# Rounded weight halves on ScalarE, a reordered first batch and a planner with measured durations, in a fused attention and expert kernel

## The chip, the cores and the metric

The kernel runs on one core of a Trainium2 chip. The metric is the device time of one execution in microseconds; lower is better. TensorE (PE) multiplies, VectorE (DVE) and ScalarE (ACT) do elementwise work, GpSimd (POOL) does some of it and issues accumulating DMAs, SyncE (SP) issues the other DMAs.

## What is computed

Two stages. First an attention over 8 batches, 8 heads, 576 positions and 64 features per head: a coarse attention on q, k and v averaged over groups of four positions, repeated four times, plus a local one in which each position sees those less than four away. Then a feed-forward stage on the 4608 rows of 512 features, with a rational activation.

```python
q_d = q.reshape(B, H, Sd, factor, D).mean(axis=3)      # k_d, v_d alike
out_d = sm_attn(q_d, k_d, v_d)
out_up = np.repeat(out_d, factor, axis=2)
mask = np.abs(pos[:, None] - pos[None, :]) < factor
...
out_local = np.matmul(attn, v)
x = (out_up + out_local), rows b*576+s, columns h*64+d
h = x @ w_in                                  # 512 -> 2048
P = a[0] + a[1] * h + a[2] * h2 + a[3] * h3
Q = 1.0 + np.abs(b[0]) * np.abs(h) + np.abs(b[1]) * h2
out = (P / (Q + 1e-06)) @ w_out               # 2048 -> 512
```

The weights come as 64-bit numbers, so that a chunk of 128 x 512 of them is 512 KB.

## The kernel before

**Planner.** Nothing is issued at once. Each piece of work is a task given to `Plan.add` (line 86) with an engine, a duration, what it reads and writes, and sometimes a due time. `Plan.run` (line 117) walks back from due times to a latest time for each task, then simulates five engines: whenever an engine is free, it takes, of its tasks that are ready by the simulated clock, the one with the earliest latest time. The result is a fixed order per engine; on the chip each engine works through its list in order, and waits where an input is not there. An engine is never held free for a task that will be ready soon. `gap` gives the time from the end of a task to the start of one that depends on it; a DMA on SP counts as 2.0 us after its issue, one on POOL as given by `lag`.

**Weights.** There are 16 chunks of w_in and 16 of w_out (`weights`, line 303). A chunk is loaded as raw words into one of eleven landing buffers (`spots`), which lie over memory used later: five over the buffers of the activation, four over the last two chunks' places, two over x. ScalarE scales one word (line 320), VectorE puts the two words together into a float (lines 323 and 326), which is kept in the place `low`. `parts` (line 337) then splits it in two: POOL rounds the high part (line 340), VectorE subtracts it to leave the low part (line 343). For w_out this follows at once; for w_in it waits until block 0 has used the whole float.

**Attention.** A batch has four pairs of heads. A pair needs qk (590 KB), vw (the windows of v, 320 KB), and pooled qk and v. For batches 1 to 7 the pooling is done by DMA: one load and three accumulating loads from POOL (line 376). For batch 0 VectorE pools qk (line 387), and v of all four pairs is pooled by one load and three accumulating ones into one buffer `vf` (lines 807 and 811). Then: scores (lines 399, 409, 426), maxima on VectorE (441, 471), exponentials on ScalarE (456, 482), normalization on VectorE (493 to 517), transposes (530, 537), copies on ScalarE (543, 553, 554), products with v (`weighted`, lines 568 and 579), and additions that put the result into x (line 611). Batch 0 is worked in two halves of two pairs; its loads on SP are interleaved with the first six weight chunks by due times. Pairs 2 and 3 of batch 0 use memory that lies over places of later chunks.

**Feed-forward.** Rows come in blocks: 512 rows of a batch, and twice 256 rows left over from four batches. A block has 16 steps (8 for the small ones), 144 steps in all. A step has `h_part` (x by one chunk of w_in), `middle` (the activation: six ScalarE operations at line 705 and seven VectorE operations at lines 720 to 738) and, two steps later, `o_part` (by one chunk of w_out, line 757). Block 0 takes w_in and x as whole floats, four slow matmuls to a step (line 680); later blocks take high and low parts, three products, twelve matmuls (line 692); for that `split_x` first splits x (lines 659 and 662). h has two PSUM banks, the output four, so that the third h step needs the first bank emptied by `middle`. The due time of step n is `due_h(n)`: `H0` for the first, `H_FIRST` more for each step of block 0 and `H_STEP` afterwards. A block's x is due `SPLIT_EARLY` before its first step. Batch 1's attention runs during block 0.

**Filling.** Where the plan leaves PE idle before the first h step, `warm` puts in matmuls with no use (line 889), for 0.6 of the planned gap.

Of the kernel before, what the change touches and what calls it, by code (L numbers as in the profile page):

```python
# [20 lines left out]
P = 128  # L21
# [51 lines left out]
class Task:  # L73
    __slots__ = ("engine", "dur", "fn", "due", "preds", "succs", "late", "start", "end", "n", "lag")


class Plan:

    LAG = {"PE": 0.25, "DVE": 0.14, "ACT": 0.18, "POOL": 0.2, "SP": 2.0}
    OWN = {"PE": 0.0, "DVE": 0.08, "ACT": 0.1, "POOL": 0.1, "SP": 2.0}
# [6 lines left out]
    def add(self, engine, dur, fn, reads=(), writes=(), due=None, lag=None):  # L89
        t = Task()  # L90
        t.engine, t.dur, t.fn, t.due, t.n = engine, dur, fn, due, len(self.tasks)
        t.lag, t.preds, t.succs, t.late, t.start = lag, {}, [], 1e9, None
# [11 lines left out]
        for k in rk - wk:  # L104
            self.readers[k].append(t) if k in self.readers else self.readers.__setitem__(k, [t])
# [6 lines left out]
    def gap(self, p, t):  # L112
        if p.lag is not None:
            return p.lag
        return (self.OWN if p.engine == t.engine else self.LAG)[p.engine]

    def run(self):
# [6 lines left out]
        waiting = {e: [] for e in self.LAG}  # L124
        open_ = {e: [] for e in self.LAG}
        free = dict.fromkeys(self.LAG, 0.0)

        def release(t):
            at = 0.0
# [7 lines left out]
        done = []  # L137
        while len(done) < len(self.tasks):
            best = None
            for e in self.LAG:  # L140
                if open_[e]:
                    at = free[e]
                elif waiting[e]:
                    at = max(free[e], waiting[e][0][0])
                else:
                    continue
                if best is None or at < best[0]:
                    best = at, e
            at, e = best
            while waiting[e] and waiting[e][0][0] <= at + 1e-9:  # L150
                t = heapq.heappop(waiting[e])[2]
                heapq.heappush(open_[e], (t.late, t.n, t))
            t = heapq.heappop(open_[e])[2]
# [14 lines left out]
def attention_moe(  # L168
# [95 lines left out]
    slots += [Slot(2 + i, high[i][half].at) for i in range(2)]  # L264
    vf = put("vf", [KC, NPAIR, 2, 2, D], F32, low[0][half].at)
# [3 lines left out]
    spots += [put(f"sl{i}", [P, 2 * DM], I32, a[w][NFC - 2].at) for i, (a, w) in enumerate(((high, 0), (low, 0), (high, 1), (low, 1)))]  # L269
    spots += [put(f"sx{i}", [P, 2 * DM], I32, xs[1][0].at + i * 4096) for i in range(2)]  # L270
# [23 lines left out]
    add("SP", 0.4, lambda: nc.sync.dma_start(out=maskb.ap, in_=mask), (), (maskb,), due=-20.0)  # L294

    def setup_coef():
        add("SP", 0.1, lambda: nc.sync.dma_start(out=cf.ap[:, :6], in_=coef), (), (cf,), due=30.0)
# [7 lines left out]
    def weights(w, f, spot, due=None):  # L305
# [25 lines left out]
        add("SP", 1.4, load, (), (spot,), due=due)  # L331
# [3 lines left out]
        if w:  # L335
            parts(w, f)

    def parts(w, f, due=None):
        hi, lo, word = high[w][f], low[w][f], bits[w][f]
        add("POOL", 1.0, lambda: nc.gpsimd.tensor_copy(out=hi.ap, in_=word.ap.bitcast(F32)), (lo,), (hi,), due=due)  # L340
# [19 lines left out]
    def load_qk(c, due=None):  # L360
        s, b, i = c.slot, c.b, c.i
        add("SP", 1.6, lambda: nc.sync.dma_start(out=s.qk.ap, in_=qk[b, i]), (), (s.qk,), due=due)

    def load_vw(c, due=None):
        s, b, i = c.slot, c.b, c.i
        add("SP", 0.9, lambda: nc.sync.dma_start(out=s.vw.ap, in_=vw[b, i]), (), (s.vw,), due=due)

    def load_pooled(c):

        s, b, i = c.slot, c.b, c.i  # L370
        for dst, src, cost in ((s.pq, qkp, 0.5), (c.vp, vp, 0.4)):
            add("SP", cost, lambda d=dst, x=src: nc.sync.dma_start(out=d.ap, in_=x[b, 0, :, i]), (), (dst,))
            for r in range(1, POOL):
                add(
                    "POOL", 1.0,
# [3 lines left out]
                    (dst,), (dst,), lag=2.8,  # L379
# [11 lines left out]
    def scores(c, bk):  # L391
# [24 lines left out]
        add("PE", 1.0, issue, (s.qk, identb, maskb), bk)  # L416

    def scores_pooled(cs, bk):
# [14 lines left out]
        add("PE", 0.9, issue, [c.slot.pq for c in cs], bk)  # L433
# [122 lines left out]
    def vp_of(c):  # L556
        return vf.ap[:, c.i] if c.b == 0 else c.vp.ap

    def weighted(cs, bk, due):
# [15 lines left out]
        def part_b():  # L575
            for c, x in zip(cs, avb):
                for kc in range(2):
                    for j in range(2):
                        nc.tensor.matmul(  # L579
                            x.ap[j * D : (j + 1) * D, 256 : 256 + SD],  # L580
                            lhsT=vp_of(c)[:, j, kc, :],
                            rhs=c.slot.ept.ap[:, kc, :, c.pos(j), :],
                            start=(kc == 0), stop=(kc == 1), skip_group_check=True,
# [10 lines left out]
        pooled_v = [vf if c.b == 0 else c.vp for c in cs]  # L594
# [25 lines left out]
        add("PE", 1.4 if len(cs) == 2 else 0.87, part_b, [c.slot.ept for c in cs] + pooled_v + ready, avb)  # L620
# [11 lines left out]
        add("PE", 0.95, part_a, ready, ava)  # L632
# [35 lines left out]
    def h_part(n, f):  # L668
# [5 lines left out]
        if k == 0:  # L674

            x = xsf[blk.slot][1]
            for c in range(NCC):
# [7 lines left out]
                add("PE", 0.88, issue, (low[0][fc], part(x, None, 4 * c * t, 4 * t)), (ph,), due=due_h(n) + 0.05 * c)  # L685
# [21 lines left out]
    def middle(n):  # L707
# [20 lines left out]
        act(0.54, tq, log, log.ap, AF.Exp, scale=-1.0)  # L728
        add("DVE", 0.61, lambda: v.tensor_tensor(out=gh.ap, in0=ta.ap, in1=tq.ap, op=ALU.mult), (ta, tq), (gh,))  # L729
# [10 lines left out]
    def o_part(n, f):  # L740
# [5 lines left out]
        due = due_h(n) + O_LAG * H_STEP + 0.25 * f  # L746
        order = [[(m, sub) for m in range(3)] for sub in range(blk.nsub)]
# [21 lines left out]
    def store(k):  # L769
        blk = blocks[k]  # L770
        due = due_h(blk.first + blk.nstep + 2)
        for sub in range(blk.nsub):
# [9 lines left out]
            for i, (b, t, n) in enumerate(rows):  # L782
# [5 lines left out]
                    (room,), (), due=due + 2,  # L788
# [4 lines left out]
    spot_of = [spots[i % 9] for i in range(9)] + [spots[5 + i % 4] for i in range(len(order) - 9)]  # L793
    late = [i for i, (w, f) in enumerate(order) if f >= NFC - 2]
    for n, i in enumerate(range(late[0], len(order))):
        spot_of[i] = spots[9 + n % 2]
    chunks = [(w, f, spot) for (w, f), spot in zip(order, spot_of)]


    c0 = [Pair(p) for p in range(NPAIR)]  # L800
    due0 = due_h(0) - 4.0
# [5 lines left out]
    add("SP", 0.8, lambda: nc.sync.dma_start(out=vf.ap, in_=vp[0, 0]), (), (vf,), due=-18)  # L807
    for r in range(1, POOL):
        add(
            "POOL", 1.0,  # L810
            lambda r=r: nc.gpsimd.dma_start(out=vf.ap, in_=vp[0, r], accum_op=ALU.add),
            (vf,), (vf,), lag=4.0,
        )
    early = (-16, -13, -10, -9, -7, -5)
    for (w, f, spot), due in zip(chunks[: len(early)], early):
        weights(w, f, spot, due)
    bk = banks
    for q in range(2):
        cs = c0[2 * q : 2 * q + 2]
        for i, c in enumerate(cs):  # L820
            scores(c, bk[2 * i : 2 * i + 2])
            softmax_local(c, bk[2 * i : 2 * i + 2])
        for c in cs:
            pool_qk(c)
        sp = bk[4:6] if q == 0 else bk[0:2]
        scores_pooled(cs, sp)
        for c, y in zip(cs, sp):
            softmax_pooled(c, y)
        for i, c in enumerate(cs):
            normalize(c)  # L830
            turned(c, [bk[n] for n in ((6, 4, 5), (6, 4, 5), (2, 3, 0), (6, 1, 2))[2 * q + i]])
        weighted(cs, [bk[n] for n in ((4, 5, 4, 5), (1, 2, 0, 3))[q]], due0 - 10.0 * (1 - q))
    for w, f, spot in chunks[len(early) :]:
        weights(w, f, spot)

    def attend(b):
# [145 lines left out]
```

## Time and profile before

| | us |
|---|---|
| median of 3 runs | 995.44 (995.34 to 995.81) |
| profiled execution, span | 992.7 |
| first h step of block 0 starts | 47.03 |
| block 1 starts | 178.56 |
| last PE matmuls start | 986.25 |

The profile is one execution on the chip. Its page gives busy times of the engines, the span in 40 slices, and groups of instructions by line; the trace behind it can be asked for stretches, instructions in order of time, and waits. L680 is line 680. Matmul records overlap, so a pitch is taken from start to start. A task's records carry the line of the operation, so L705 stands for all six ScalarE operations of the activation. Rows of DMA queues show bytes and the time to landing.

### The profile page before, as it was taken

To read this page: it belongs to the slowest core of one execution; us is meant where nothing else is said; L and a number is where in the kernel's file an instruction comes from. 1 tells how busy PE (TensorE), PEld (TensorE's weight loads), DVE (VectorE), ACT (ScalarE), POOL (GpSimd) and SP (SyncE) were. 2 spreads that over 40 slices of the span, in tenths; PEclk is the share of its full clock that TensorE was granted. 3 is DMA by queue.
4 is the path that set the end of the run, shared out by engine and by line. 5 is a ranking of instruction groups with operands and counts; after the bars stand their busy time and mean duration, and the time that the engine had idled before them with its cause. 6 is when DMAs were issued, how large, how long until landed. Compare 5 with 4: busy or idle time off the path is not lost.

```text
span 992.7 us, 19799 instructions
## 1 busy us (share of the span) xinstructions
PE 961.0 (97%) x7365; PEld 758.1 (76%) x7365; DVE 849.1 (86%) x1472; ACT 796.6 (80%) x2046; POOL 180.4 (18%) x209
## 2 busy tenths in 40 slices
PE   6689998999999999999999999999999999999997
PEld 5545665788888878987878887887878888898886
DVE  6799999989778988887887898888888898888886
ACT  6578768797979798779787988798797979767675
POOL 1523543222221213001303030302122220000000
PEclk9999999999999999999999999999999999999999
DMA  9963553433342324002424242533334320100001
GB/s 322 281 210 120 118 158 70 117 68 74 74 125 51 74 74 84 34 22 74 75 72 96 85 80 59 95 96 56 92 57 112 74 52 1 44 1 22 1 1 42
DMA packets 46371, 83.43 MB, mean 84 GB/s; under 512 B 6564, under 2 KB 29092, under 8 KB 46276
## 3 DMA queue, kind: packets, MB, share of 16 engines
q1 hardware_dynamic: 25828, 62.70, 19.1%
q0 software_dynamic: 20448, 19.48, 14.1%
q8 instruction: 58, 0.95, 0.4%
q14 instruction: 37, 0.30, 0.1%
HBM read 72.72 MB, written 9.44 MB: 83 GB/s over the span
## 4 chain that ended last, share of the span: by engine, by line
PE 82%; DVE 10%; DMA 4%; issue 2%; POOL 1%; SPq 1%; ACT 1%; ACTq 0%; DVEq 0%; POOLq 0%
PE psum L757 36%; PE psum L692 36%; PE psum L568 2%; DMA pq<-in_qkp_dram 2%; PE psum L579 1%; PE psum L530 1%; PE psum L537 1%; PE psum L409 1%; PE psum L426 1%; DMA qk<-in_qk_dram 1%; DVE m L720 1%; DMA sx<-in_w_out_dram 1%; DVE m L726 1%; POOL wh L340 1%; DVE g L729 1%
## 5 line engine op out<-in xcount | busy, mean ns | idle before, releaser
L757 PE MATMUL psum<-wh,g 128*128 128x512 f32 x1152 | 371.7, 403 | 4.7 <-DVE g L738 2.7
L692 PE MATMUL psum<-xs,wh 128*128 128x512 f32 (+1 forms) x1152 | 265.2, 370 | 0.0
L705 ACT ACTIVATE m<-psum,cf 128x512 f32<-128x512 f32 x288 | 217.5, 759 | 51.9 <-PE psum L692 41.9
L757 PEld LDWEIGHTS psum<-wh,g 128*128 128x128 f32 x1152 | 209.3, 188 | 55.5 <-issue 7.7
L692 PEld LDWEIGHTS psum<-xs,wh 128*128 128x128 f32 x1152 | 199.3, 188 | 35.9
L757 PE MATMUL psum<-wl,g 128*128 128x512 f32 x576 | 225.0, 392 | 0.0
L705 ACT ACTIVATE gb<-psum,cf 128x512 f32<-128x512 f32 x144 | 115.7, 803 | 53.9 <-PE psum L757 53.7
L376 POOL DMA_DIRECT2D pq<-in_qkp_dram x84 | 73.9, 913 | 398.3 <-DMA pq<-in_qkp_dram 312.5
L692 PE MATMUL psum<-xs,wl 128*128 128x512 f32 (+1 forms) x576 | 141.5, 367 | 0.0
L729 DVE TENSOR_TENSOR g<-m,m 128x512 fp32r<-128x512 f32 x144 | 100.6, 699 | 43.2 <-ACT m L705 41.3
L720 DVE SCALAR_TENSOR_TENSOR m<-m,cf,m 128x512 f32<-128x512 f32 x144 | 108.9, 756 | 31.2 <-ACT m L705 31.1
L757 PEld LDWEIGHTS psum<-wl,g 128*128 128x128 f32 x576 | 108.4, 188 | 23.4
L456 ACT ACTIVATE el<-psum,nm 128x64 f32<-128x64 f32 x320 | 97.0, 345 | 30.4 <-DVE nm L448 30.1
L726 DVE TENSOR_TENSOR m<-m,gb 128x512 f32<-128x512 f32 x144 | 101.7, 706 | 20.3 <-ACT gb L705 16.3
L692 PEld LDWEIGHTS psum<-xs,wl 128*128 128x128 f32 x576 | 101.3, 189 | 18.9 <-issue 1.2
L705 ACT ACTIVATE gb<-m,cf 128x512 f32<-128x512 f32 x144 | 107.0, 743 | 6.3 <-DVE m L720 6.3
L732 DVE SCALAR_TENSOR_TENSOR m<-m,g 128x512 f32<-128x512 f32 x144 | 100.0, 695 | 2.9
L737 DVE TENSOR_TENSOR m<-m,m 128x512 f32<-128x512 f32 x144 | 99.2, 689 | 2.8
L376 POOL DMA_DIRECT2D vp<-in_vp_dram x84 | 72.7, 925 | 154.5 <-DMA vp<-in_vp_dram 136.8
L725 DVE TENSOR_TENSOR m<-m,m 128x512 f32<-128x512 f32 x144 | 98.5, 684 | 0.5 <-ACT m L705 0.5
L738 DVE TENSOR_TENSOR g<-m,m 128x512 fp32r<-128x512 f32 x144 | 97.9, 680 | 0.8
L705 ACT ACTIVATE m<-gb 128x512 f32<-128x512 f32 x144 | 93.6, 650 | 3.5 <-DVE m L725 0.9
(66 smaller groups left out, 999.0 us busy)
## 6 DMA issues: line engine op xcount, KB each, us to landing
qk<-in_qk_dram SPq DMA_DIRECT2D x32, 590.0 KB, 8.0
pq<-in_qkp_dram POOLq DMA_DIRECT2D x84, 144.0 KB, 3.3
vw<-in_vw_dram SPq DMA_DIRECT2D x32, 320.0 KB, 4.0
out_dram<-xf SPq DMA_DIRECT2D x32, 256.0 KB, 2.4
vp<-in_vp_dram POOLq DMA_DIRECT2D x84, 72.0 KB, 3.0
sl<-in_w_in_dram SPq DMA_DIRECT2D x10, 512.0 KB, 4.7
sl<-in_w_out_dram SPq DMA_DIRECT2D x10, 512.0 KB, 6.3
pq<-in_qkp_dram SPq DMA_DIRECT2D x28, 144.0 KB, 2.2
```

Source lines behind the costliest of these rows:

```text
L376: lambda d=dst, x=src, r=r: nc.gpsimd.dma_start(out=d.ap, in_=x[b, r, :, i], accum_op=ALU.add),
L456: nc.scalar.activation(out=s.el.ap[:, k, c.pos(j), :], in_=view[:, j, k, :], func=AF.Exp, bias=nm[:, 5 * j + k : 5 * j + k + 1], scale=sca ...
L692: nc.tensor.matmul(ph.ap[:, f * t : (f + 1) * t], lhsT=(high, low)[j][0][fc].ap[:, c, :], rhs=blk.x[i].ap[:, c, :], start=(part_ == 0 and ...
L705: add("ACT", cost, lambda: nc.scalar.activation(out=out_.ap, in_=in_, func=func, **kw), (room_in, cf, *more), (out_,))
L720: lambda: v.scalar_tensor_tensor(out=tb.ap, in0=tq.ap, scalar=b1, in1=tb.ap, op0=ALU.mult, op1=ALU.add),
L725: add("DVE", 0.61, lambda: v.tensor_tensor(out=ta.ap, in0=ta.ap, in1=tq.ap, op=ALU.mult), (ta, tq), (ta,))
L726: add("DVE", 0.61, lambda: v.tensor_tensor(out=ta.ap, in0=ta.ap, in1=u.ap, op=ALU.add), (ta, u), (ta,))
L729: add("DVE", 0.61, lambda: v.tensor_tensor(out=gh.ap, in0=ta.ap, in1=tq.ap, op=ALU.mult), (ta, tq), (gh,))
L732: lambda: v.scalar_tensor_tensor(out=tb.ap, in0=tb.ap, scalar=CONE, in1=gh.ap.bitcast(F32), op0=ALU.add, op1=ALU.mult),
L737: add("DVE", 0.61, lambda: v.tensor_tensor(out=tb.ap, in0=ta.ap, in1=tb.ap, op=ALU.subtract), (ta, tb), (tb,))
L738: add("DVE", 0.61, lambda: v.tensor_tensor(out=gl.ap, in0=tb.ap, in1=tq.ap, op=ALU.mult), (tb, tq), (gl,))
L757: nc.tensor.matmul(ob[sub].ap, lhsT=g[i].ap[:, f0 : f0 + P], rhs=flat((high, low)[j][1][fc].ap), start=(fc == 0 and m == 0), stop=(fc == N ...
```

## The change

- **High parts.** `parts` rounds the high part with a ScalarE copy instead of a GpSimd one; planned duration 0.5 instead of 1.0.
- **First batch.** All qk loads come first, then pooled v, then vw, then the weight chunks; there are no due times on them. Pooled v goes into two buffers, each by one load and one accumulating load, and the product sums over both. The pairs are worked one at a time, each with banks given by `FIRST`, and due `PAIR_GAP` apart.
- **Planner.** Durations are changed to other values, DMAs get a delay that follows their size, an engine is free from 0.7 on. New is the hold: where a task of earlier latest time (by `HOLD_MARGIN`) will be ready before 0.7 of the chosen task has passed, the engine takes a ready task that fits in the time until then, or is left free; this up to a planned time of 54.4.
- **Landing buffers.** The two over x go; the four shared ones now lie over the high places of w_in chunks 14, 5, 3 and 1 (and each one's successor).
- **Batch 1's loads** are not planned before 45 (first two pairs) and 75 (others).
- **Due times** are changed by constants. The code for `n < WHOLE` (w_out as whole floats in the first steps) is there, with WHOLE = 0.

```diff
-        add("POOL", 1.0, lambda: nc.gpsimd.tensor_copy(out=hi.ap, in_=word.ap.bitcast(F32)), (lo,), (hi,), due=due)
+        add("ACT", 0.5, lambda: nc.scalar.copy(out=hi.ap, in_=word.ap.bitcast(F32)), (lo,), (hi,), due=due)
...
-        if p.lag is not None:
-            return p.lag
+        if p.load is not None:
+            return 2.05 if p.engine == "SP" else 1.8 + 1.3 * p.load
...
-            t = heapq.heappop(open_[e])[2]
+            t = ready[e][0][2]
+            urgent = None
+            for r, _, w in waiting[e]:
+                if r < at + t.dur * HOLD and w.late < t.late - HOLD_MARGIN and (urgent is None or w.late < urgent[0]):
+                    urgent = w.late, r
+            if urgent is not None and at < HOLD_UNTIL:
+                fits = [x for x in ready[e] if at + x[2].dur <= urgent[1] + 0.05]
+                if not fits:
+                    free[e] = urgent[1]
+                    continue
+                x = min(fits)
+                ready[e].remove(x)
+                heapq.heapify(ready[e])
+                t = x[2]
...
-    slots += [Slot(2 + i, high[i][half].at) for i in range(2)]
-    vf = put("vf", [KC, NPAIR, 2, 2, D], F32, low[0][half].at)
+    slots += [Slot(2 + i, high[i][half - 1].at) for i in range(2)]
+    vf = [put(f"vf{i}", [KC, NPAIR, 2, 2, D], F32, low[0][half + 2 * i].at) for i in range(2)]
...
-    spots += [put(f"sl{i}", [P, 2 * DM], I32, a[w][NFC - 2].at) for i, (a, w) in enumerate(((high, 0), (low, 0), (high, 1), (low, 1)))]
-    spots += [put(f"sx{i}", [P, 2 * DM], I32, xs[1][0].at + i * 4096) for i in range(2)]
+    spots += [put(f"sl{i}", [P, 2 * DM], I32, high[0][(NFC - 2, half - 3, half - 5, half - 7)[i]].at) for i in range(4)]
...
-        add("SP", 1.4, load, (), (spot,), due=due)
+        add("SP", 1.28, load, (), (spot,), due=due, load=1.28)
...
-                for kc in range(2):
+                terms = [(v, kc) for kc in range(2) for v in vp_of(c)]
+                for n, (v, kc) in enumerate(terms):
...
-    for c, due in zip(c0, (-19, -17, -15, -12)):
-        load_qk(c, due)
-    for c, due in zip(c0, (-14, -11, -8, -6)):
-        load_vw(c, due)
+    for c in c0:
+        load_qk(c)
+    for r in range(POOL):
+        v = vf[r // 2]
+        if r % 2:
+            add(
+                "POOL", 0.93, lambda r=r, v=v: nc.gpsimd.dma_start(out=v.ap, in_=vp[0, r], accum_op=ALU.add),
+                (v,), (v,), load=1.3,
+            )
+        else:
+            add("SP", 0.8, lambda r=r, v=v: nc.sync.dma_start(out=v.ap, in_=vp[0, r]), (), (v,), load=0.8)
+    for c in c0:
+        load_vw(c)
...
-    for q in range(2):
-        cs = c0[2 * q : 2 * q + 2]
...
+    for i, c in enumerate(c0):
+        sc, sp, tb, av = FIRST[i]
+        scores(c, [banks[n] for n in sc])
+        softmax_local(c, [banks[n] for n in sc])
+        pool_qk(c)
+        scores_pooled([c], [banks[sp]])
+        softmax_pooled(c, banks[sp])
+        normalize(c)
+        turned(c, [banks[n] for n in tb])
+        weighted([c], [banks[n] for n in av], due_h(0) - 1.0 - PAIR_GAP * (NPAIR - 1 - i))
...
-                load_qk(c), load_pooled(c), load_vw(c)
+                at = HOLD_LOADS[q] if b == 1 else 0.0
+                load_qk(c, at), load_pooled(c, at), load_vw(c, at)
...
-                    parts(0, n, due_h(n + blocks[0].nstep) - 2.0)
+                    parts(0, n, due_h(n + blocks[0].nstep) - PARTS_EARLY)
...
-H0 = 40.0
-H_FIRST = 8.0
+H0 = 36.0
+H_FIRST = 6.73
 H_STEP = 6.2
-SPLIT_EARLY = 6.0
+SPLIT_EARLY = 9.51
+PARTS_EARLY = 14.42
 QUAD_GAP = 45.0
+PAIR_GAP = 3.53
+COEF = 16.26
+HOLD = 0.7
+HOLD_MARGIN = 2.06
+HOLD_UNTIL = 54.4
 WARM = 0.6
+WHOLE = 0
+HOLD_LOADS = (45.0, 75.0)
```

More of the change, by code (lines that the diff above doesn't have):

```diff
@@ L73 @@
 class Task:
-    __slots__ = ("engine", "dur", "fn", "due", "preds", "succs", "late", "start", "end", "n", "lag")
+    __slots__ = ("engine", "dur", "fn", "due", "preds", "succs", "late", "start", "end", "n", "load", "at")
 class Plan:
-    LAG = {"PE": 0.25, "DVE": 0.14, "ACT": 0.18, "POOL": 0.2, "SP": 2.0}
-    OWN = {"PE": 0.0, "DVE": 0.08, "ACT": 0.1, "POOL": 0.1, "SP": 2.0}
+    ENGINES = ("PE", "DVE", "ACT", "POOL", "SP")
+    LAG = {"PE": 0.25, "DVE": 0.14, "ACT": 0.18, "POOL": 0.2}
+    OWN = {"PE": 0.0, "DVE": 0.08, "ACT": 0.1, "POOL": 0.1}
     def __init__(self):
@@ L123, in run @@
         left = {t: len(t.preds) for t in self.tasks}
-        waiting = {e: [] for e in self.LAG}
-        open_ = {e: [] for e in self.LAG}
-        free = dict.fromkeys(self.LAG, 0.0)
+        waiting = {e: [] for e in self.ENGINES}
+        ready = {e: [] for e in self.ENGINES}
+        free = dict.fromkeys(self.ENGINES, 0.7)
+        done = []
         def release(t):
-            at = 0.0
+            at = t.at
             for p in t.preds:
@@ L136, in run @@
                 release(t)
-        done = []
         while len(done) < len(self.tasks):
             best = None
-            for e in self.LAG:
-                if open_[e]:
+            for e in self.ENGINES:
+                if ready[e]:
                     at = free[e]
@@ L334, in weights @@
         add("DVE", 0.6, lower, (spot, lo), (lo,))
-        if w:
+        if w and f >= WHOLE:
             parts(w, f)
@@ L618, in put_x @@
             )
[L620 removed]
+        add("PE", 1.6, part_b, [c.slot.ept for c in cs] + pooled_v + ready, avb)
         for c, x in zip(cs, avb):
@@ L746, in o_part, with issue @@
         due = due_h(n) + O_LAG * H_STEP + 0.25 * f
+        if n < WHOLE:
+            x = gb[n % 2]
+            for sub in range(blk.nsub):
+                def issue(sub=sub):
+                    nc.tensor.matmul(
+                        ob[sub].ap, lhsT=x.ap[:, sub * P : (sub + 1) * P], rhs=flat(bits[1][fc].ap).bitcast(F32),
+                        start=(fc == 0), stop=False,
+                    )
+                add("PE", 0.858, issue, (x, low[1][fc]), (ob[sub],), due=due + 0.02 * sub)
+            return
         order = [[(m, sub) for m in range(3)] for sub in range(blk.nsub)]
@@ L787, in store @@
                     ),
-                    (room,), (), due=due + 2,
+                    (room,), (), due=due + 2, load=0.7,
                 )
     order = sorted(((w, f) for w in range(2) for f in range(NFC)), key=lambda c: c[1] / 2 + 1.5 * c[0])
[L793 to L796, printed above, removed]
@@ L833, in attention_moe @@
-    for w, f, spot in chunks[len(early) :]:
+    chunks = [(w, f, spots[i if i < 9 else 5 + (i - 9) % 4]) for i, (w, f) in enumerate(order)]
+    c0 = [Pair(p) for p in range(NPAIR)]
+    for c in c0:
[3 more added lines that the diff above has]
+        if r % 2:
+            add(
+                "POOL", 0.93, lambda r=r, v=v: nc.gpsimd.dma_start(out=v.ap, in_=vp[0, r], accum_op=ALU.add),
+                (v,), (v,), load=1.3,
+            )
+        else:
+            add("SP", 0.8, lambda r=r, v=v: nc.sync.dma_start(out=v.ap, in_=vp[0, r]), (), (v,), load=0.8)
@@ L874, in attention_moe @@
                 o_part(o, f)
+                if k == 0 and o < WHOLE:
+                    parts(1, o, due_h(o + blocks[0].nstep) + O_LAG * H_STEP - PARTS_EARLY)
             if s == blocks[k].nstep - 1:
```

93 lines of the change are left out of this document (43 added, 50 removed), and 4 rows, old and new, of the table FIRST.

## The prediction

> **What bounds the kernel now.** I read the page first, its busy times and its slices; then the table by stretches; then TensorE's instructions in order of time, to place the cuts; then what ScalarE, VectorE and GpSimd did there; last, the instruction groups.
>
> ```profile
> span 992.7 us, 19799 instructions
> PE 961.0 (97%) x7365; PEld 758.1 (76%) x7365; DVE 849.1 (86%) x1472; ACT 796.6 (80%) x2046; POOL 180.4 (18%) x209
> PE   6689998999999999999999999999999999999997
> ```
>
> 97% for PE is an average. The slices show where the remainder is: at the start, and a little at the end. The stretches are cut where the first h step starts (47.03), where the third starts (59.06), where the last h step of block 0 ends (162.5) and where block 1 starts (178.56). The columns are PE, PEld, DVE, ACT and POOL busy, then granted clock, DMA share and GB/s.
>
> ```profile
> 0.00:47.03 47.03, 32.07 (x561) 23.96 (x562) 33.31 (x72) 29.88 (x136) 14.53 (x24) 1.00 0.95 301
> 47.03:59.06 12.03, 9.64 (x60) 4.29 (x60) 9.20 (x17) 5.88 (x10) 4.26 (x6) 0.86 1.05 334
> 59.06:162.50 103.44, 98.06 (x572) 58.25 (x572) 101.83 (x179) 83.50 (x227) 41.14 (x41) 1.00 0.47 127
> 162.50:178.56 16.06, 12.58 (x138) 9.59 (x137) 15.43 (x28) 11.13 (x23) 3.82 (x5) 0.89 0.35 64
> 47.03:178.56 131.53, 120.28 (x769) 72.13 (x769) 126.46 (x221) 100.52 (x258) 49.23 (x50) 0.97 0.51 138
> 178.56:992.70 814.14, 808.67 (x6037) 661.99 (x6035) 689.31 (x1181) 666.20 (x1652) 116.65 (x136) 1.00 0.27 63
> ```
>
> ```profile
> 47.03 8.80 PE L680 MATMUL psum<-xf,wb 128*128 128x512 f32 x16 [3.89 <-DVE xf L611]
> 59.06 7.23 PE L680 MATMUL psum<-xf,wb 128*128 128x512 f32 x16 [2.38 <-ACT gb L705]
> 178.56 2.88 PE L692 MATMUL psum<-xs,wh 128*128 128x512 f32 x12
> ```
>
> From 178.56 on PE is busy 808.67 of 814.14 us, and its work there is the same after the change. So the question is **how much earlier block 1 starts**. Before it VectorE is the full engine: 101.83 of 103.44 in the long middle stretch. PE itself does real work at this rate:
>
> ```profile
> 95.65 3.59 PE L680 MATMUL psum<-xf,wb 128*128 128x512 f32 x8
> 184.00 0.62 PE L757 MATMUL psum<-wh,g 128*128 128x512 f32 x2
> 186.72 1.98 PE L692 MATMUL psum<-xs,wh 128*128 128x512 f32 x8
> ```
>
> An h step of block 0 is the eight records of the first row, 3.59 us; an o step is the twelve matmuls between the other two, 2.72 us.
>
> **The change part by part.**
>
> *First batch ahead of the weights, pair by pair.* On SP, ten loads (four qk, four vw, two of pooled v) and two accumulating loads on POOL go ahead of every chunk load. By the DMA view of the first 48 us (count, size, us to landing) they are 4 x (590 + 320 + 288) KB = 4.8 MB:
>
> ```profile
> qk<-in_qk_dram SPq DMA_DIRECT2D x6, 590.0 KB, 8.5
> vw<-in_vw_dram SPq DMA_DIRECT2D x6, 320.0 KB, 11.8
> vf<-in_vp_dram POOLq DMA_DIRECT2D x3, 288.0 KB, 7.8
> ```
>
> At the first stretch's 301 GB/s that is 16 us, so the first chunk lands near 18 us. That costs nothing: h needs it only after 35 us, and it has twenty us of cover. What is removed shows on VectorE, and where ScalarE starts:
>
> ```profile
> 8.65 0.31 ACT L456 ACTIVATE el<-psum,nm 128x64 f32<-128x64 f32 x1 [6.64 <-DVE nm L448]
> 17.43 1.35 DVE L387 TENSOR_REDUCE pq<-qk 128x288 f32<-128x1152 f32 x1 [1.74 <-DMA qk<-in_qk_dram]
> 40.95 0.69 DVE L343 TENSOR_TENSOR wl<-wb,wh 128x512 fp32r<-128x512 f32 x1 [2.22 <-POOL wh L340]
> 42.50 1.07 DVE L323 TENSOR_SCALAR wb<-sx 128x512 int32<-128x512 int32 x1
> 46.32 1.67 DVE L611 TENSOR_TENSOR xf<-psum,up 128x48 f32<-128x48 f32 x6
> ```
>
> The fourth pair's qk came 1.74 us late; VectorE stood 2.22 us at a subtraction whose POOL cast was not done; and 3.82 us of weight work (42.50 to 46.32) ran ahead of the additions that give h its x. Together 7.8 us, which puts the first h step at 39.2. Bounds: nothing, and from below ScalarE, which starts its exps at 8.65 and is busy 29.88 us up to 47.03, 1.3 of them a table load and 6.8 ten chunk scalings (0.68 each); 8.65 + 21.8 + 1.7 for the last additions = 32 us, a gain of 15. I take 7.8, the waits I can name. Pooled v in two buffers adds 16 matmuls of about 0.075 us (sixteen take 1.20 at L579), beside idle PE, and shortens three loads in sequence, which nobody waits for at the end: zero.
>
> *The first two h steps.* They took 12.03 us where two steps are 7.2. TensorE was at half clock, and ScalarE, in order, stood at chunk scalings whose loads were late before it could empty the first h bank:
>
> ```profile
> 48.00:49.00 1.00, 1.00 (x2) 0.37 (x2) 0.65 (x2) 0.28 (x1) 0.82 (x1) 0.50 0.87 303
> 47.61 0.67 ACT L320 ACTIVATE sl<-sl 128x512 f32<-128x512 f32 x1 [5.28 <-DMA sl<-in_w_out_dram]
> 55.91 0.70 ACT L320 ACTIVATE sx<-sx 128x512 f32<-128x512 f32 x1 [1.40 <-DMA sx<-in_w_out_dram]
> 56.52 0.66 ACT L705 ACTIVATE m<-psum,cf 128x512 f32<-128x512 f32 x1
> ```
>
> The holds and the loads of batch 1 put off to 45 and 75 take other traffic away from these chunks. Bounds 0 and 4.8 us; I take 4.0, near the upper, because five late loads in a row need the DMA queue as full as it is now (0.95 and 1.05), and batch 1's loads were part of that fullness (two of the six qk and two of the six vw loads above). What comes late next is VectorE.
>
> [...] PE stood idle for 3.89 us up to 47.03 and then ran at 0.50. [...]
>
> *High parts on ScalarE.* 32 casts leave POOL, 32 copies join ScalarE. The rows: groups up to 200 us, and, for L726, L720 and L729, a second time from 800 to 900 (x16 and x17); then instructions in order of time.
>
> ```profile
> L340 POOL CAST wh<-wb 128x512 fp32r<-128x512 f32 x32 | 35.5, 1175 | 55.8 <-DVE wb L326 55.8
> L343 DVE TENSOR_TENSOR wl<-wb,wh 128x512 fp32r<-128x512 f32 x32 | 23.7, 746 | 3.8 <-POOL wh L340 3.8
> L726 DVE TENSOR_TENSOR m<-m,gb 128x512 f32<-128x512 f32 x19 | 15.4, 813 | 0.0
> L738 DVE TENSOR_TENSOR g<-m,m 128x512 fp32r<-128x512 f32 x18 | 12.2, 680 | 0.0
> L726 DVE TENSOR_TENSOR m<-m,gb 128x512 f32<-128x512 f32 x16 | 11.0, 690 | 3.5 <-ACT gb L705 3.2
> L720 DVE SCALAR_TENSOR_TENSOR m<-m,cf,m 128x512 f32<-128x512 f32 x20 | 16.3, 813 | 0.4 <-ACT m L705 0.4
> L720 DVE SCALAR_TENSOR_TENSOR m<-m,cf,m 128x512 f32<-128x512 f32 x17 | 12.7, 747 | 3.5 <-ACT m L705 3.5
> L729 DVE TENSOR_TENSOR g<-m,m 128x512 fp32r<-128x512 f32 x19 | 14.3, 754 | 0.6 <-ACT m L705 0.6
> L729 DVE TENSOR_TENSOR g<-m,m 128x512 fp32r<-128x512 f32 x16 | 11.0, 691 | 5.5 <-ACT m L705 5.2
> 59.11 3.23 POOL L340 CAST wh<-wb 128x512 fp32r<-128x512 f32 x5
> 59.72 3.17 DVE L726 TENSOR_TENSOR m<-m,gb 128x512 f32<-128x512 f32 x1
> 176.84 1.17 ACT L659 CAST xs<-xf 128x512 fp32r<-128x512 f32 x2 [2.35 <-DVE xf L611]
> ```
>
> The two rows at 59 us show the conflict: while five casts run, one VectorE instruction takes 3.17 us. Early, L726 has a mean of 813 ns; late, without casts, 690: 19 x 0.123 = 2.3 us. L720 in the same way 20 x 0.066 = 1.3, L729 19 x 0.063 = 1.2; L343 against L738 (both write fp32r) 32 x 0.066 = 2.1. So VectorE gets back 6.9 us, some 6 of them in the middle stretch, where most casts run. ScalarE pays: two copies of this shape back to back take 1.17, so one adds about 0.55; 24 fall in the middle stretch, 13 us, and ScalarE goes from 83.5 to 96.5 of 103.44. Bounds for the stretch: 6 us gained, or 6 lost if half of what ScalarE takes on lands ahead of a step. I take 3 gained, half of what VectorE gets back, since ScalarE has 7 us left and is then almost as full as VectorE. Behind each copy, which waits for VectorE's lower words, ScalarE's queue holds the activations that empty the h banks, and PE waits for these.
>
> *Due dates and the last stretch.* Between 162.5 and 178.56 no h step can run, since block 1's x is not ready: 3.48 us idle and about 1.8 lost at half clock (0.89 granted over 16.06). The x work now has dates 3.5 us earlier before each block. Bounds 0 and 5.3; I take 2.
>
> *What is paid back.* h starts 7.8 us earlier, so the 3.82 us of weight work that ran before it fall into a stretch where VectorE is full, unless they fit into its 13.7 idle us of the first 47. Half: -2. The high parts' earlier dates pull two subtractions forward (0.6 each); the four shared landing buffers hold back the parts of chunks 1, 3, 5 and 14 until the last chunk has passed. Both are beside other work as long as chunks end before block 1; no term. The branches for n < WHOLE never run, since WHOLE is 0.
>
> **Sum:** 7.8 + 4.0 + 3.0 + 2.0 - 2.0 = 14.8 us; block 1 starts at 163.8, the span is 977.9. The median of the runs, 995.44, lies 2.7 above the span; so 980.6. Cross-check by VectorE: from its first qk at 6.06, its 33.31 + 126.46 - 6.9 us without a gap end at 158.9, a gain of at most 20.
>
> **The rivals.**
>
> *Full recovery.* VectorE runs almost without a gap from the first load: block 1 at 159 to 160, 975 to 977 as time. For it: 13.7 idle us before 47, the holds. Against: three engines would be at 97% with a fixed order.
>
> *ScalarE becomes the bound.* Its 13 us land ahead of the activations that empty the h banks; the middle stretch grows by 2 instead of shrinking by 3, and nothing is won at its end. 7.8 + 4 - 2 - 2 = 7.8: time 988. For it: ScalarE is at 93% already before anything shrinks, and it works in order. Against: it had 20 idle us.
>
> *The start does not move.* The order assumes 1.28 us for a 512 KB chunk, which is 410 GB/s; the row of the first stretch has 301. Chunks arrive late, ScalarE stands at their scalings again, with first-batch exps behind. Then only the casts and the end count, some 5 us: 990.
>
> *Slower: block 1's x comes late.* Batch 1's loads stand behind chunk loads on SP, which wait for four landing buffers emptied by a full VectorE; SP's two chunk loads here span 8 us for that reason:
>
> ```profile
> 110.37 8.07 SPq L310 DMA_DIRECT2D sl<-in_w_in_dram  x2
> ```
>
> The point from which it decides is x ready for 178.56: if batch 1's attention ends later than now, block 1 starts later by as much whatever the start won; 8 us later, one such hold, gives a time of 1003. Against: the loads of its second half now lie 60 us ahead of their use, so even at 75 there is cover.
>
> **How the numbers follow.** Forecast 0.50, full recovery 0.13, ScalarE 0.15, no earlier start 0.13, slower 0.09. The forecast's terms alone spread it over 975 to 987. The range, 971 to 991, takes in both gain rivals and reaches most of the one whose start stays; outside are the slower case and the far ends of the others, under 0.2. About 0.2%, 2 us, is what a measurement of this kernel tells from no change. Within 0.2%: 0.03, from the tails of the two small gains; slower 0.09; faster 0.88.
>
> **What would show each step.** The first L680 matmul near 39, not 47. The first ScalarE activation of a middle (L705) within 3 us of the end of the first h step, with no chunk scaling's DMA wait ahead of it. No VectorE instruction of 1 us or more among the middles; L726's early mean at 690. ScalarE at 95% or less between third h step and block 1; if it is fuller and PE waits for it, its rival holds. The first L692 near 164. The stretch from there to the end still 814 us: a change there would make the whole sum wrong.

## The result

The changed kernel takes 985.03 us (982.67 to 986.21, 4 runs) where the kernel before took 995.39 beside it: a ratio of 0.9904, 95% interval 0.9881 to 0.9927. Run once more beside other runs of the kernel before, it gave 0.9884 (0.9869 to 0.9899). So it is about 1% faster, 10 to 11 us. The forecast was 14.8 us, a time of 980.6.

The page of the changed kernel, the lines that answer to those shown of before: span, busy time and PE's slices.

```profile
span 983.4 us, 19740 instructions
PE 961.4 (98%) x7343; PEld 759.8 (77%) x7343; DVE 836.5 (85%) x1472; ACT 811.8 (83%) x2078; POOL 147.5 (15%) x176
PE   6999999999999999999999999999999999999997
```

Then its stretches, cut at the same events: first h matmul (35.07), third h step (57.93), block 1 (164.43). Columns as before. The fence behind it has PE's matmuls in order of time: those of h (L695), the end of the fourth pair's product with v (L582), and the start of block 1. Lines have moved. For TensorE L680 is now L695, L692 L707, L757 L802, L568 L582 and L409 L423; the rounding of the high parts, L340, is L354; for VectorE L343 is now L357, L720 L735 and L726 L741; ScalarE's L705 is L720. The last row but one is from the scores of a pair of batch 2.

```profile
0.00:35.07 35.07, 25.52 (x417) 20.55 (x418) 21.19 (x46) 22.60 (x101) 2.52 (x8) 0.95 0.84 281
35.07:57.93 22.86, 18.77 (x140) 10.62 (x139) 17.70 (x39) 14.57 (x49) 0.00 (x0) 0.78 0.52 177
57.93:164.43 106.50, 105.64 (x785) 65.43 (x785) 104.69 (x197) 102.68 (x270) 29.18 (x34) 1.00 0.68 176
164.43:983.40 818.97, 811.51 (x6011) 663.22 (x6004) 692.93 (x1193) 671.90 (x1661) 115.81 (x135) 1.00 0.27 62
```

```profile
35.07 1.88 PE L695 MATMUL psum<-xf,wb 128*128 128x512 f32 x4
37.26 1.99 PE L695 MATMUL psum<-xf,wb 128*128 128x512 f32 x4 [0.31 <-ACT el L470]
...
45.38 1.91 PE L695 MATMUL psum<-xf,wb 128*128 128x512 f32 x2
...
49.34 2.39 PE L582 MATMUL psum<-et,vw 64*64 64x58 f32 x40
51.66 4.52 PE L695 MATMUL psum<-xf,wb 128*128 128x512 f32 x6
57.93 3.70 PE L695 MATMUL psum<-xf,wb 128*128 128x512 f32 x8 [1.75 <-ACT gb L720]
...
163.75 0.75 PE L423 MATMUL psum<-qk 64*64 64x64 f32 x40
164.43 3.04 PE L707 MATMUL psum<-xs,wh 128*128 128x512 f32 x12
```

Three things are to be seen. **h starts at 35, but only with half of its columns.** The eight records at 35 and 37 are the first two column groups of the first and of the second h step, which need the first two pairs of heads; the other eight come at 45 and 51.66, when the third and fourth pair are done. The third h step starts at 57.93 against 59.06: 1.1 us earlier. **From there to block 1 it takes 106.50 us where it took 119.50** (59.06 to 178.56): PE idle 0.9 us instead of 8.9. That is where the gain is. **The rest takes 4.8 us longer**, 818.97 against 814.14. Part of that is work that crossed the mark. Up to block 1 the trace of before has 180 matmuls of o steps, that of after 168: one o step of 2.72 us was put off behind the mark. The other way, the scores of one pair of batch 2 came ahead of it (360 matmuls of L423 where L409 has 320), which takes 0.84 us, from 163.59 to 164.43. Counted for equal work, the long stretch is 11.1 us shorter and not 13.0, and some 3 us of the 4.8 remain. PE waits 1.4 us of these for ScalarE (at 179.70), and the remainder is spread thin.

VectorE's groups up to 200 us (names, shapes, count, busy, mean ns) and ScalarE's new copies up to 190:

```profile
L741 DVE TENSOR_TENSOR m<-m,gb 128x512 f32<-128x512 f32 x20 | 13.7, 686 | 0.3
L735 DVE SCALAR_TENSOR_TENSOR m<-m,cf,m 128x512 f32<-128x512 f32 x21 | 15.6, 745 | 2.0 <-ACT m L720 2.0
L357 DVE TENSOR_TENSOR wl<-wb,wh 128x512 fp32r<-128x512 f32 x32 | 21.2, 681 | 0.7 <-ACT wh L354 0.7
L354 ACT CAST wh<-wb 128x512 fp32r<-128x512 f32 x32 | 20.3, 667 | 0.0
```

The means are those that the kernel before had only where no cast ran (690 for L741, 747 for L735), and L357 is down from 746.

### The profile page after: what moved, and what is told of

It is laid out like the page before. It is cut to its first block, busy times and chain, and to the rows that moved or that the text cites. A ratio compares the mean times of both kernels' runs of the same rounds, so it can differ in the third digit from the quotient of the medians.

```text
span 983.4 us, 19740 instructions
## 1 busy us (share of the span) xinstructions
PE 961.4 (98%) x7343; PEld 759.8 (77%) x7343; DVE 836.5 (85%) x1472; ACT 811.8 (83%) x2078; POOL 147.5 (15%) x176
## 4 chain that ended last, share of the span: by engine, by line
PE 88%; ACT 7%; DMA 2%; DVE 1%; issue 1%; SPq 0%; ACTq 0%; DVEq 0%
PE psum L802 38%; PE psum L707 36%; PE psum L582 2%; PE psum L695 2%; PE psum L594 2%; ACT m L720 2%; PE psum L551 2%; PE psum L544 2%; PE psum L423 1%; PE psum L440 1%; ACT el L470 1%; DMA qk<-in_qk_dram 1%; DMA sl<-in_w_out_dram 1%; ACT gb L720 1%; ACT sl L334 1%
## 5 line engine op out<-in xcount | busy, mean ns | idle before, releaser
L802 PE MATMUL psum<-wh,g 128*128 128x512 f32 x1152 | 369.5, 402 | 0.5 <-issue 0.4
L720 ACT ACTIVATE m<-psum,cf 128x512 f32<-128x512 f32 x288 | 218.0, 757 | 63.1 <-PE psum L707 58.2
L707 PE MATMUL psum<-xs,wh 128*128 128x512 f32 (+1 forms) x1152 | 267.3, 370 | 1.4 <-ACT gb L720 1.4
L802 PEld LDWEIGHTS psum<-wh,g 128*128 128x128 f32 x1152 | 209.4, 188 | 50.1 <-issue 5.5
L707 PEld LDWEIGHTS psum<-xs,wh 128*128 128x128 f32 x1152 | 199.0, 189 | 38.3 <-ACT gb L720 2.0
L802 PE MATMUL psum<-wl,g 128*128 128x512 f32 x576 | 224.5, 391 | 0.0
L720 ACT ACTIVATE gb<-psum,cf 128x512 f32<-128x512 f32 x144 | 116.2, 807 | 55.6 <-PE psum L802 55.6
L707 PE MATMUL psum<-xs,wl 128*128 128x512 f32 (+1 forms) x576 | 142.7, 370 | 0.0
L802 PEld LDWEIGHTS psum<-wl,g 128*128 128x128 f32 x576 | 108.1, 188 | 23.7
L735 DVE SCALAR_TENSOR_TENSOR m<-m,cf,m 128x512 f32<-128x512 f32 x144 | 107.4, 746 | 15.7 <-ACT m L720 15.1
L741 DVE TENSOR_TENSOR m<-m,gb 128x512 f32<-128x512 f32 x144 | 99.1, 688 | 24.0 <-ACT gb L720 20.9
L707 PEld LDWEIGHTS psum<-xs,wl 128*128 128x128 f32 x576 | 100.5, 189 | 18.6 <-issue 1.2
L720 ACT ACTIVATE gb<-m,cf 128x512 f32<-128x512 f32 x144 | 107.9, 749 | 0.7 <-DVE m L735 0.7
L720 ACT ACTIVATE m<-gb 128x512 f32<-128x512 f32 x144 | 93.6, 650 | 3.0
```

What stands on the lines that cost most here:

```text
L707: nc.tensor.matmul(ph.ap[:, f * t : (f + 1) * t], lhsT=(high, low)[j][0][fc].ap[:, c, :], rhs=blk.x[i].ap[:, c, :], start=(part_ == 0 and ...
L720: add("ACT", cost, lambda: nc.scalar.activation(out=out_.ap, in_=in_, func=func, **kw), (room_in, cf, *more), (out_,))
L735: lambda: v.scalar_tensor_tensor(out=tb.ap, in0=tq.ap, scalar=b1, in1=tb.ap, op0=ALU.mult, op1=ALU.add),
L741: add("DVE", 0.61, lambda: v.tensor_tensor(out=ta.ap, in0=ta.ap, in1=u.ap, op=ALU.add), (ta, u), (ta,))
L802: nc.tensor.matmul(ob[sub].ap, lhsT=g[i].ap[:, f0 : f0 + P], rhs=flat((high, low)[j][1][fc].ap), start=(fc == 0 and m == 0), stop=(fc == N ...
```

## The experiments

All are compared with the kernel before on the same chip; the figures are medians, the ratio with its 95% interval.

| kernel | us | ratio to before |
|---|---|---|
| changed | 985.03 | 0.9904 (0.9881 to 0.9927) |
| changed, again | 982.66 | 0.9884 (0.9869 to 0.9899) |
| changed, casts on GpSimd | 993.87 | 0.9998 (0.9985 to 1.0011) |
| changed, old due times | 988.62 | 0.9948 (0.9933 to 0.9963) |
| changed, batch 1's loads not held | 984.86 | 0.9911 (0.9887 to 0.9936) |
| changed, no filling | 985.20 | 0.9924 (0.9897 to 0.9952) |
| changed, no filling, no holds | 985.80 | 0.9916 (0.9899 to 0.9932) |
| before, casts on ScalarE | 991.24 | 0.9965 (0.9950 to 0.9980) |
| before, new due times | 987.88 | 0.9940 (0.9925 to 0.9954) |
| before, both of these | 982.48 | 0.9887 (0.9869 to 0.9906) |
| changed, 12 more fillers | 982.79 | 0.9884 (0.9866 to 0.9903) |
| the same, fillers on another bank | 980.03 | 0.9859 (0.9839 to 0.9878) |
| changed, only the other bank | 980.57 | 0.9859 (0.9842 to 0.9875) |

**Casts back on GpSimd.** The question was why the stretch from the third h step to block 1 had become 13 us shorter.

```diff
-        add("ACT", 0.5, lambda: nc.scalar.copy(out=hi.ap, in_=word.ap.bitcast(F32)), (lo,), (hi,), due=due)
+        add("POOL", 1.0, lambda: nc.gpsimd.tensor_copy(out=hi.ap, in_=word.ap.bitcast(F32)), (lo,), (hi,), due=due)
```

> The changed kernel with one part undone: the high parts are rounded on GpSimd again (planned at 1.0 us as before); all else stays, the planner draws up the order for it. Theory A, the casts on GpSimd held VectorE up and their removal is what shortened the stretch from the third h step to block 1 (119.5 us before, 106.5 after): five us or more of the 10 are given back, a time of 990 or more, with VectorE instructions of 1 to 3 us among the activations. Theory B, that stretch became shorter by the new due times and the order of batch 1's attention: 2 us at most are given back, 985 to 987. Undecided between: 987 to 990.

The whole gain is gone. The stretches of that version, third and last, and two of VectorE's groups in the third:

```profile
52.72:169.96 117.24, 109.23 (x740) 67.35 (x741) 111.37 (x195) 94.30 (x249) 55.96 (x54) 0.97 0.65 169
169.96:991.80 821.84, 813.16 (x6049) 663.68 (x6047) 697.01 (x1197) 670.25 (x1656) 122.01 (x141) 1.00 0.27 62
```

```profile
L735 DVE SCALAR_TENSOR_TENSOR m<-m,cf,m 128x512 f32<-128x512 f32 x14 | 11.9, 850 | 0.1
L357 DVE TENSOR_TENSOR wl<-wb,wh 128x512 fp32r<-128x512 f32 x13 | 10.1, 779 | 4.4 <-POOL wh L354 4.4
```

The stretch takes 117.24 instead of 106.50, 10.7 us more. VectorE's busy time makes 6.7 of these (111.37 against 104.69): its instructions take longer, as the means of 850 and 779 ns show against 745 and 681 in the changed kernel. The other 4.1 are VectorE standing idle (5.9 against 1.8 us); of the 5.9, 4.4 are a single wait for a cast, which GpSimd does late. Another 2.9 us come behind block 1 (821.84 against 818.97). The span grows by less than the sum of these, by 8.4 us, since the third h step comes at 52.72 here; this profile has a granted clock of 1.00 from 45 to 55 us, where the changed kernel's has 0.50. Theory A holds for the changed kernel.

**Each part alone in the kernel before.** First the casts (the edit above, the other way), then the due times, then both.

```diff
-H0 = 40.0
-H_FIRST = 8.0
+H0 = 36.0
+H_FIRST = 6.73
...
-SPLIT_EARLY = 6.0
+SPLIT_EARLY = 9.51
```

> The kernel before with one part of the change alone: the high parts rounded by ScalarE (planned at 0.5 us). Theory A: five us or more faster than the kernel before, 990 or less, VectorE's mean for L726 near 690 ns up to 200 us. Theory B: within 2 us of 995; VectorE is freed but block 1's x is still due when it was, so block 1 still starts near 178.

> The kernel before with the new due times alone (36, 6.73, 9.51), casts still on GpSimd. Casts alone gave 0.35%, casts and due times together 1.13%. Theory E, each part needs the other: VectorE, full with the casts' delays, can't meet earlier dates, so the dates alone give 2 us at most (992 to 996). Theory F, the two add up: the dates alone give about 8 us (986 to 988).

> The kernel before with two parts of the change: casts on ScalarE, and the new due times (36, 6.73 and 9.51 in place of 40, 8 and 6); first batch, loads and planner durations as before. With the casts alone the h steps of block 0 ended 5.2 us sooner (157.46 against 162.64), but block 1 waited for its x until 175.84. Theory C, the freed time was held back by late x, and the due times release it: block 1 starts at 171 or sooner, time 988 or less. Theory D, x is late because the old order plans with wrong durations and not because of its dates: block 1 stays within 2 us of 175.8, time 990 to 992.

Casts alone give 0.35%, 3.5 us, between the two theories. VectorE is freed, as theory A has it: the mean of L726 is 684 ns up to 200 us. The stretch shows why not more comes of it: the h steps of block 0 end at 157.46, 5.2 us sooner than before, but block 1 starts at 175.84 only. In the 18 us between, PE has only batch 1's attention and o steps to do. It is idle for 4.9 us of them, and the granted clock is 0.82 on the mean. The second row is this time, the first the whole stretch from the third h step; then PE at the end of it:

```profile
58.48:175.84 117.36, 111.86 (x705) 69.65 (x706) 112.26 (x210) 103.06 (x269) 19.54 (x22) 0.95 0.46 123
157.46:175.84 18.38, 13.45 (x133) 10.01 (x132) 15.74 (x29) 13.57 (x28) 6.06 (x7) 0.82 0.43 87
```

```profile
170.47 1.39 PE L568 MATMUL psum<-et,vw 64*64 64x58 f32 x64 [2.00 <-DVE xf L611]
...
175.84 1.21 PE L692 MATMUL psum<-xs,wh 128*128 128x512 f32 x4
```

Due times alone give 0.60%, 6 us. The time of 987.88 lies in theory F's range, and the gain is somewhat below its 8 us. Both together give 1.13%, 11 us: the sum of the two is 9.5, and the difference is within the intervals. It is as much as the whole change gives. With both, the stretch is that of the changed kernel although nothing of its first batch, durations or holds is in it:

```profile
46.85:57.57 10.72, 9.64 (x60) 4.29 (x60) 8.54 (x16) 7.12 (x13) 2.54 (x3) 0.84 1.07 341
57.57:163.20 105.63, 104.81 (x740) 65.12 (x741) 104.01 (x197) 101.17 (x266) 18.74 (x21) 1.00 0.49 133
163.20:980.00 816.80, 811.07 (x6009) 663.51 (x6004) 688.13 (x1189) 669.83 (x1655) 116.23 (x136) 1.00 0.27 63
```

So theory C holds: the casts free VectorE, and the due times bring batch 1's attention forward, between h and o steps, so that x is ready when the h steps end. The last product with v of batch 1 starts at 159.45 here, at 170.47 with the casts alone. Which of the three constants does it was not tried. The first h step starts at 46.85, 11.8 us after the changed kernel's, and the third at 57.57.

**Old due times in the changed kernel.**

```diff
-H0 = 36.0
-H_FIRST = 6.73
+H0 = 40.0
+H_FIRST = 8.0
...
-SPLIT_EARLY = 9.51
-PARTS_EARLY = 14.42
+SPLIT_EARLY = 6.0
+PARTS_EARLY = 2.0
```

> The changed kernel with the old due times (40, 8, 6 and 2 in place of 36, 6.73, 9.51 and 14.42). Theory C: block 1's x comes late again behind the last h step, block 1 starts 4 to 10 us later than 164.4, time 988 to 994. Theory D: within 2 us of the changed kernel (983 to 987).

Half of the gain goes, 4 to 6 us. Block 1 starts at 168.00, 3.6 us later, just short of theory C's 4, and with one o step more ahead of it (180 matmuls); the time lies in theory C's range. The last h step ends at 153.55: again 14 us in which x is late, as theory C has it. In the changed kernel some 5 us lie between the two. PE fills most of the 14 us with o steps and attention:

```profile
153.55:168.00 14.45, 11.97 (x177) 8.16 (x175) 14.06 (x29) 14.30 (x30) 5.17 (x6) 1.00 0.47 85
```

**Loads not held, no filling, no holds.**

```diff
-HOLD_LOADS = (45.0, 75.0)
+HOLD_LOADS = (0.0, 0.0)
```

> The changed kernel without the earliest times of 45 and 75 for batch 1's loads. If they keep the DMA queue free for chunks: chunk scalings on ScalarE wait for their loads again, third h step later than 57.93, 2 to 5 us slower. If the chunks are early enough anyway (they wait for landing buffers, not for the queue): within 1.5 us of the changed kernel.

```diff
-WARM = 0.6
+WARM = 0.0
```

> The changed kernel without any idle-filling matmuls. In the changed kernel 13 of them start at 21.66, after a wait of 2.21 us for a bank that ScalarE was still to empty, and run 2.88 us at half clock, while VectorE waits 3.88 us for the pooled scores behind them. If they cost the chain more than the clock they keep is worth: the fourth pair's scores come 3 us earlier than 33.48 and the time falls by 1 to 3 us. If the clock counts for more: TensorE at 0.5 through the first 55 us, and 1 to 4 us slower.

```diff
-HOLD_UNTIL = 54.4
+HOLD_UNTIL = 0.0
...
-WARM = 0.6
+WARM = 0.0
```

> The changed kernel without holds, and without idle-filling matmuls (which would write over a bank in use in this order); to be read against the version without filling, 985.2. If the holds do what they are for: the last pair's work is late behind chunk work, third h step later than 59.14, 2 to 5 us slower than 985.2. If the start's gain doesn't hang on them: 984 to 987.

None of the three can be told from the changed kernel by its time. Holding batch 1's loads is worth nothing that shows here, and so are the holds, though without them the third h step came at 63.20, not 59.14: 4 us at the start that were made up behind it (block 1 at 167.91 against 169.41). The version without filling had runs from 984.3 to 990.3, and its profile is of the slowest. In it PE ran at 0.70 of its clock up to the first h matmul at 39.21, and the fourth pair's scores came at 37.55, 4 us later and not 3 us earlier. With the fillers the granted clock up to the first h matmul was higher, 0.95 up to 35.07 in the changed kernel's first profile and 0.90 up to 35.93 in its second, and yet the time gains nothing that shows. The next runs show where it is lost.

**The fillers.** In the changed kernel 13 filling matmuls stand in PE's queue at 21.66, ahead of the last transpose of the first pair. They write to bank 7, which ScalarE has still to empty. So they don't fill the wait of 2.21 us, they run after it, for 2.88 us and at a granted clock of 0.50 (21.66 to 24.38); the third pair's pooled scores (L440) stand behind them:

```profile
21.66 2.88 PE L924 MATMUL psum<-maskb,identb 128*128 128x256 bf16 x13 [2.21 <-ACT ept L557]
24.38 0.27 PE L551 MATMUL psum<-ident,el 128*128 128x128 f32 x1
...
25.71 0.95 PE L440 MATMUL psum<-pq 64*64 64x144 f32 x12
```

Three versions: 12 more fillers between the first and last column group of the first h step; these and the 13 sent to bank 5, which is free then; and the second edit alone. The 12 more write to bank 6. Of the first version's edit this is the part that reaches to the last column group:

```diff
...
-        if t.due is not None and t.due == due_h(0):
+        if t.due is not None and abs(t.due - due_h(0) - 0.05 * (NCC - 1)) < 1e-6:
             break
```

> The changed kernel with 12 more idle-filling matmuls, put where the plan leaves TensorE idle between the first and the last column group of the first h step (35 to 52 us). In the changed kernel TensorE runs at half clock from 44.9 to about 55 us, and the third h step starts at 57.93. If the clock holds and that stretch is bound by TensorE: clock 1.00 there, third h step near 53.5, time 981. If 12 small matmuls don't hold the clock, or ScalarE and VectorE bound the stretch: within 1 us of the changed kernel.

> The version with 12 more idle-filling matmuls (982.8), and in it the 13 filling matmuls that waited for bank 7 write to bank 5, which is free then, so they run in the wait and not after it. If the 2.9 us that they took lay on the chain of the first batch: VectorE's wait of 3.88 for the pooled scores shrinks to 1 or so, first h step near 33.5, third near 52, time 980 to 981.5. If ScalarE's work is the chain: the start moves by less than 1 us and the time stays at 982 to 984.

The edit of the third version:

```diff
-            nc.tensor.matmul(banks[7].ap[:, : 2 * P], ...
+            nc.tensor.matmul(banks[5 if n == 13 else 7].ap[:, : 2 * P], ...
```

> The changed kernel with one edit: the 13 filling matmuls that stood behind bank 7 write to bank 5; the 12 additional ones are not there. If the bank alone made the version of 980.0 faster: 980 to 981.5, a ratio of 0.985 to 0.987, first h step near 33. If the 12 additional ones are needed to keep the clock from 45 us on: 982 to 985 in some or all runs, with a granted clock of 0.5 somewhere between 40 and 55 us in the profile.

The 12 more decide nothing. Their version kept its clock (1.00 from 35.98 to 54.37), with the third h step at 54.37 and 982.8 us; but the changed kernel, run again, kept it without them (1.00 from 35.93 to 54.13), with the third h step at 54.13 and 982.7. The bank alone is worth what the two edits are together. In the third version the fillers run in the wait, the pooled scores come two us earlier, and the third h step starts at 51.76:

```profile
19.47 1.58 PE L924 MATMUL psum<-maskb,identb 128*128 128x256 bf16 x13
21.84 0.33 PE L551 MATMUL psum<-ident,el 128*128 128x128 f32 x1 [0.79 <-ACT ept L557]
...
23.72 0.95 PE L440 MATMUL psum<-pq 64*64 64x144 f32 x12
```

It takes 980.57 us, 0.9859 (0.9842 to 0.9875): 14 us less than the kernel before and 2 to 4 less than the changed one. The interval just overlaps with that of the changed kernel's second group of runs (0.9869 to 0.9899). But of the eight runs with bank 5, with and without the 12 more, the slowest took 981.27, and of the eight runs of the changed kernel only one (980.84) was below that.

**The changed kernel again.**

> The changed kernel as it is, once more, beside these runs of the kernel before: 983 to 986, a ratio of 0.990 to 0.992. Anything else would mean that the figures of different groups of runs can't be set side by side.

Both came out better than expected: 982.66 is below 983, and the ratio of 0.9884 lies outside 0.990 to 0.992. By the expectation this means that figures of different groups of runs can't be set side by side as closely as that, although the intervals of the two ratios overlap. What differs in the two profiles just ahead of the third h step is the clock from 45 to 55 us, 0.50 in the first and 1.00 in the second (from 20 to 30 us it is the other way, 0.83 and 0.67). The first two rows are of the first profile, the other two of the second:

```profile
45.00:50.00 5.00, 4.89 (x31) 2.99 (x33) 3.09 (x6) 1.33 (x4) 0.00 (x0) 0.50 0.74 238
50.00:55.00 5.00, 5.00 (x38) 3.06 (x35) 3.49 (x8) 1.91 (x4) 0.00 (x0) 0.50 0.48 179
```

```profile
45.00:50.00 5.00, 4.04 (x61) 2.84 (x61) 4.42 (x11) 3.48 (x9) 0.00 (x0) 1.00 0.56 195
50.00:55.00 5.00, 3.24 (x8) 1.17 (x7) 4.83 (x9) 4.13 (x8) 0.00 (x0) 1.00 0.87 269
```

One program, two courses: with the low clock there the third h step starts at 57.93 and the span is 983.4, without it 54.13 and 980.5. The mean clock of each run fits this. Ten us at half clock take 0.005 off the mean over the span; of the eight runs, three have a mean of 0.991 or 0.992 and took 984.9 to 986.2, and five have 0.995 or 0.996 and took 980.8 to 983.8. Where the low clock fell in the runs without a profile is not known. So a comparison of versions of this kernel by less than 3 us needs the clock of that place beside it.

## Why the prediction was right, and where it was not

The direction, the range and the mark at block 1 (163.8 forecast, 164.43 measured) came out. The terms did not, and that the sum is near is luck: their errors went both ways. Up to the third h step 11.8 us were forecast and 1.1 measured; from there to block 1, 3.0 (the terms 3.0, 2.0 and -2.0) and 13.0, or 11.1 for equal work. For equal work the mark itself would stand at 166.3.

**First batch, 7.8, and first two h steps, 4.0: failed.** The prediction put the first h step at 39.2 and let all of that count. By the third h step 1.1 us was won, 4.9 in the run without the low clock from 45 to 55 us. It failed in taking the first h matmul for the start of a step: worked pair by pair, h begins with half its columns and stands until the fourth pair is done. The long waits that it named did go (VectorE doesn't wait for the fourth pair's qk, and the last chunk scalings before the first middle wait 0.57 and 0.41 us for their loads, not 5.28), but another took their place, the fillers behind bank 7. With that one removed the third h step starts at 51.76, 7.3 us before the old one; at the end 2 to 4 us of it are left over the changed kernel, and 0.28%, 3 us, over the casts and due times alone (0.9859 against 0.9887, with intervals that overlap). The whole rest of the change, put on top of casts and due times, gives nothing that can be measured (0.9887 without it, 0.9904 and 0.9884 with it). The rival whose start does not move had the outcome at the third h step right, but not its reason, the late chunks. The product over two buffers of pooled v added 32 matmul records and not 16 (64 of L594, where L579 has 32); its term was zero either way.

The low clock that the prediction read off the kernel before, 0.50 behind 3.89 us in which PE stood idle, was there again in the first profile, at another place: it fell inside the first step, at 44.9, and not before h. There was no such idle time in the ten us ahead of the drop; the longest gap in them was 1.06 us, before 42.74. PE had less work there (3.08 us busy from 40 to 45, against 3.93 in the profile without the drop), and then ran at 0.50 for ten us, busy for 9.89 of the 10.10 up to 55. Why the clock fell in one profile of the program and not in the other was not shown.

**High parts on ScalarE, 3.0: mis-sized.** VectorE's part was right (6 us in the stretch forecast, 6.7 measured; mean of L741 690 forecast, 686 measured). Two things were wrong in what followed. The wait of VectorE for late casts, 4.1 us in the changed order, was left out; and half of the gain was taken off for a ScalarE nearly full. A copy took 0.63 us and not 0.55 (20.3 us for 32), and ScalarE did fill up, to 102.68 of 106.50 us (96%, where the prediction had set 95% as the sign), but PE was busy 105.64 of the 106.50, so it did not become the bound. The part is worth 3.5 us in the old order, 5 on top of the new due times (0.9940 to 0.9887), and 9 to 11 in the full change. The last two are differences between groups of runs.

**Due dates, 2.0: mis-sized.** They are worth 6 us alone (4.6 to 7.5 by the interval), three times the forecast and about the upper bound of 5.3 or more. Two things were wrong. The forecast took the dates of x as 3.5 us earlier, by SPLIT_EARLY. But H0 and H_FIRST count too: in the plan, block 1's x was due at 40 + 16 x 8 - 6 = 162, and is now due at 36 + 16 x 6.73 - 9.51 = 134.2. And the bound was read off the last stretch alone, its idle time and lost clock, while attention work brought forward also fills the gaps ahead of it. In the kernel before with new due times PE is idle 4.2 us from third h step to block 1, where it was 8.9 (2.7 us of the shorter stretch are again an o step put off):

```profile
57.92:169.13 111.21, 107.05 (x696) 66.09 (x697) 110.27 (x194) 92.15 (x246) 50.06 (x48) 0.97 0.51 134
```

**Paid back, -2.0: right in sign, wrong in kind.** 4.8 us came back, not as weight work on VectorE but behind the mark: 1.9 as the o step that was put off, less the scores that came forward, 2.0 as PE standing idle longer (7.5 us against 5.5), and 1.0 as busy time that was not followed further. That the work from block 1 on is the same, and takes 814 us, was the assumption that failed; the prediction itself had named a change there as the sign that its sum is wrong.

What stays open: with casts on GpSimd, the old kernel with new due times gives 0.9940, and the changed kernel 0.9998. The rest of the change then costs 6 us; with casts on ScalarE it costs nothing. The single wait of 4.4 us for a cast may be part of it; why the order meets it was not tried. Nor was any part of the rest (pairs, durations, landing buffers, `PARTS_EARLY`) put into the kernel before alone.

## What to carry to other kernels

Count time won at the start only at a mark where equal work is done: a step begun with half its inputs, or one pushed behind the mark, looks like gain and is not. Where an engine is full, look at what its work waits for next; freeing VectorE was worth 3.5 us until the data of the next block were due earlier, and the two together 11. A filler should write where no other engine has still to read: here 13 that wrote to a bank which ScalarE had still to empty waited 2.21 us and then ran for 2.88 ahead of the work behind them, and with a free bank they ran in the wait, in 1.58.

## What the runs showed of the hardware

The same program had PE at 0.50 from 45 to 55 us in one profile and at 1.00 in another. Once low, the clock stayed so for some ten us (0.50 from 44.9 to 55), while PE had work without a gap from 45.11 on, and h matmuls took longer: six records 4.52 us at 51.66, where the version with the other bank has 2.84 at 46.31, at 1.00. From 45 to 50 us PE looks busier at 0.50 (4.89 of 5 us) than at 1.00 (4.04): here busy time alone doesn't show the low clock.

A ScalarE copy of 128 x 512 to a high part has a mean of 667 ns by its records, a cast of the same shape on GpSimd in the kernel before a mean of 1175 with 603 at the least. VectorE's waits for high parts up to 200 us came to 0.7 us in the changed kernel, and to 3.1 (copies) against 3.8 (casts) in the old order. What the move to ScalarE took away in both orders is the lengthening of VectorE's own instructions: L343 has 746 ns beside the casts and 687 with the copies in the old order; in the changed one, from the third h step to block 1, L357 has 779 beside the casts and 677 with the copies.
